# Attention with a gated Mish block: the last half groups normalised in a buffer of their own, leftover projections over three PSUM banks, and another order of the instructions

## The chip, the cores and the metric

The kernel runs on one core of a Trainium2 chip. The metric is the device time of one execution in microseconds (us). The kernel is one straight program: a planner written in Python decides, while the program is built, in which order each engine gets its instructions; on the chip the engines (TensorE = PE, ScalarE = ACT, VectorE = DVE, GpSimd = POOL, and the DMA queue of SyncE = SP) each run their own list in order and wait for each other by semaphores.

## The reference

The inputs are x (2048 x 640), weights of an attention with 32 heads of 20 columns, and weights of a dense block of 1536 columns. Only A_x is used as x.

```
x = A_x
g = sigmoid((x * gate_w).sum(-1, keepdims=True))
q, k, v = split((x @ wqkv), heads=32, width=20)
p = softmax(q @ k.T / sqrt(20))            # 32 heads, 2048 x 2048 each
a = concat(p @ v) @ wo
h = x @ w1 + b1
b = (h * tanh(softplus(h))) @ w2
out = g * a + (1 - g) * b
```

## The kernel before, in words

Four heads make a group g (0 to 7), 512 query columns a chunk c (0 to 3). The attention walks over the pairs (c, g): first chunks 0 and 1 for each g, then chunk 2 and chunk 3 through all g. A unit is 128 keys x 512 queries of one head. Three units fill a slot, three PSUM banks of scores; there are 683 slots, and two slots are in flight at a time (banks 0 to 2 and 3 to 5). Bank 6 (`ACC`) collects p @ v of the running group, bank 7 (`FB`) takes one projection task at a time.

The very last pair, (3, 7), is cut in two halves of 256 queries, which the code names (3, 7) and (3, 8), so that the first half can be finished while the second still runs.

A slot's way: PE writes its scores (`score_mms`, line 1197), ACT turns them into exp in an SBUF tile `ETS` (line 1219), PE multiplies them with V into `ACC` (`pv`, line 1456). V has a column of ones, so the row sums of the softmax arise in the same matmuls. In many slots one of the three units is taken off ACT: ACT then gets 128x1024 instead of 128x1536 elements, and DVE computes the third exp with integer and half-float tricks. That is an offloaded unit:

- line 1264 (`emit_x`): DVE reads the scores out of PSUM into an SBUF pad, 128x512, as an integer;
- lines 1328, 1332, 1336 (`close`): for a batch of up to four units, fraction, product and power, on 128x2048 elements for a full batch, 128x1024 for two and 128x512 for one (a batch of three as two plus one);
- `emit_off` then feeds both parts, "U" and "E", to PE as two V matmuls per unit.

Which slots lose a unit is decided by `choose`. It compares DVE's backlog as the planner knows it (`late`) with limits. Other work is spread around the slots: projections (`kq_task`, `pack_task`, `v_task`), the dense block (`h_task`, line 943, with Mish on ACT line 976 and DVE lines 998 and 1001; `b_task`, line 1017), the output projections (`p_task`, `part_task`, line 1041) and their mixing with the gate (`mix`, line 1047). `pick` takes the next task for PE in due order. `fill_up` puts in matmuls without use (`spin`, line 1735, and `repeat_s`) where PE would stream for too small a share of a window; `SPUN` and `STREAM` are the shares.

When a group's last matmul into `ACC` is done, `group_done` has DVE copy `ACC` to `OUNG` (line 1538), which frees `ACC` for the next group; the sums are inverted (line 1545), spread over partitions by DMA through DRAM (`SUMS`, `BCT`), and DVE multiplies (line 1506). The two last halves are normalised without DMA: copy, transpose, reciprocal, transpose, multiply on DVE (lines 1523 to 1531). The first half keeps its copy in `OUNG`, and needs `OUNG`, `BCT` and `RR` free, so the normalisation of group (3, 6), which uses the same buffers, is put ahead of it. The second half is read straight from PSUM.

For chunk 3 the sum over groups 0 to 5 is projected early (`part_task`, into `PART`, a part of `W2R`). Groups 6 and 7 follow: for the first 256 queries as `p_task` with rest=True (four tasks of two matmuls, each mixed by DVE into `HB` and stored), for the second 256 queries in four jobs after everything else, of which three are mixed by DVE, and one by ACT (line 1862) and POOL (line 1864). All of these four `p_task`s use bank 7.

Of the kernel before, what the change touches and what calls it, by code (L numbers as in the profile page):

```python
# [17 lines left out]
P = 128  # L18
# [5 lines left out]
NG = 8  # L24
# [4 lines left out]
NC = 4  # L29
CW = 512  # L30
NHC = 8
HW = 256
# [8 lines left out]
SLOT = 3  # L41
# [12 lines left out]
PASS = CW * COL  # L54
EXP = 1.335
STREAM = 0.5
SPUN = 0.65
EXP_PAIR = 0.908
WIDE = 0.60
QUICK = 0.335  # L60
# [39 lines left out]
WINDOW = 3.41  # L100
CALM = 3
# [8 lines left out]
THIN = 0.09  # L110
REFILL = 0.58
OVER = 0.2
CUTS = ((0, 256), (256, 256))

# [14 lines left out]
EXPONENT = 0x7C00  # L129
HALVES = 0x3800  # L130
WARM = 7
MORE = 8


# [108 lines left out]
def bass_gated_mix__softmax_full_mha__dense_activation_mish__prompt_kernel(  # L243
# [142 lines left out]
    def attention(pl, fast):  # L386
# [7 lines left out]
        soon = [deque() for _ in range(LANES)]  # L394
        norm = deque()
        acts = deque()
        now = {"step": -1, "open": None, "bank": False, "rate": 9.0}


        if fast:  # L400
# [1092 lines left out]
        def group_done(c, g, step, last):  # L1493
# [15 lines left out]
                    otn_read[c % 2] = []  # L1509

            if end:
                while norm:
                    norm.popleft()[1]()
                if (c, g) == groups[-1]:
                    flush(lambda: not any(soon))
                for at, w in ([cut[(c, g)]] if fast else [(n * HW, HW) for n in range(2)]):
                    cols = slice(at, at + w)
                    src, bc, rr = PS[:, ACC, cols], BC[:, cols], RR[:, at // 32:(at + w) // 32]
                    cost = w * COL * 2.6 + 0.09
                    if (c, g) != groups[-1]:  # L1520
                        held = OUNG[:, cols]
                        last = acc_free[0] = pl.add(
                            "dve", lambda e, src=src: e.tensor_copy(held, src), [last, oung_free[0]], cost=cost)
                        src = held
                    a = pl.add("dve", lambda e, src=src, bc=bc: e.transpose(bc, src), [last, bc_read[0]], cost=cost)
                    a = pl.add("dve", lambda e, bc=bc, rr=rr, w=w: e.reciprocal(rr, bc[:, 0:w:32]), [a, rr_read[0]], cost=0.15)
# [4 lines left out]
                    end_done.append(pl.add("dve", lambda e, src=src, bc=bc, to=to: e.tensor_tensor(  # L1531
                        to, src, bc, ALU.mult), [a, *reads()], cost=cost))
                oung_free[0] = bc_read[0] = rr_read[0] = otn_done[(c, g)] = end_done[-1]
                return
            while oung_free[0] == "busy":
# [2 lines left out]
            ev = dve(lambda e: e.tensor_copy(src, PS[:, ACC, :]), [last, oung_free[0]], WIDE)  # L1538
            oung_free[0] = "busy"
            acc_free[0] = ev  # L1540
            got = pl.add("sp", lambda e: e.dma_start(
                RR[:, :], OUNG[0:P:32, :].rearrange("j (r a) -> j r a", a=16)), [ev, rr_read[0]], "nr0", cost=0.55, tail=1.4 if place[(c, g)] else SLOW_LOAD)

# [16 lines left out]
        if fast:  # L1560
# [9 lines left out]
            for g in range(NG):  # L1570
                for c in range(NC):
                    due = slot_of(0, g, 4 * c)
                    if c or g:
                        if g == 0:
                            tasks.append(kq_task(1, g, c, due - 3))
                        if g < 2:
                            tasks.append(v_task(g, c, due - 1))
                        if g == 0:
                            tasks.append(kq_task(0, g, c, slot_of(1, 0, 0) - 5 if c < 2 else Q_AT + Q_STEP * (c - 2)))
# [37 lines left out]
            parts = [part_task(t, half, NSLOT - 26) for t in range(4) for half in range(2)]  # L1617
            parts += [p_task(NC - 1, t, half, NSLOT - 2, True) for t in range(last_t[0]) for half in range(2)]
            made = []
            for make, args in rest:  # L1620
                t = make(*args, 0)
# [39 lines left out]
        def load_flag(eng, handle):  # L1661
            flags[eng] = handle.value_load(FLAG[0:1, 0:1], min_val=0, max_val=1)

        def pick(limit):

            switch = SWITCH if pl.kind != "F" else 0
            if now["open"]:
                return now["open"] if pl.now["pe"] + now["open"].cost + switch <= limit else None
            free = bank_free.get(FB)
# [12 lines left out]

        def put(task):
            now["open"] = task
            if issue(task, FB):
                now["open"] = None
                tasks.remove(task)
                if fast and task is last_kv:
                    load_w1(FIRST)
                    load_w1(FIRST + 1)  # L1690
                    area[0] = 1
                if fast and task in q_tasks:
                    q_tasks.remove(task)
                    if not q_tasks:
                        load_wo()
# [301 lines left out]
```

## Time and profile before

| what | value |
|---|---|
| time, median of 3 runs | 791.36 us (791.05 to 792.82) |
| the profiled execution's own time | 791.27 us |
| its span in the profile | 789.4 us |
| busy: ACT, DVE, PE | 773.3, 748.6, 709.7 us |
| granted TensorE clock, mean | 0.997 |

The span runs from the first to the last instruction; the profiled execution took 1.87 us more than its span. Durations in the prediction come from this one execution. A duration of a single instruction includes its fill and drain, which overlap with its neighbours; the distance between two starts is what an instruction costs in a full queue.

### The profile page before, as it was taken

The page shows a single profiled execution, that of the slowest core. Times are in us where ns is not written, and L with a number is a line of the kernel's source. Part 1 is how long each engine was busy: PE and PEld are TensorE (multiplying, and loading weights), DVE is VectorE, ACT ScalarE, POOL GpSimd, SP SyncE. Part 2 cuts the span into 40 slices and gives each one's busy share as a digit, 9 for nine tenths or more (in the row PEclk, how much of TensorE's full clock was granted, in tenths as well). Part 3 has the DMA queues.
Part 4 walks back from the last instruction along what each step waited for, and adds up shares of the span by engine and source line. Part 5 has one row for each costly group of instructions (what it writes and reads, how often), then busy time and mean ns, then how long its engine had stood idle before and what let it go on. Part 6 is the DMA issues. An engine that isn't in the chain of part 4 may idle for free.

```text
span 789.4 us, 16424 instructions
## 1 busy us (share of the span) xinstructions
PE 709.7 (90%) x6649; PEld 262.4 (33%) x6690; DVE 748.6 (95%) x1313; ACT 773.3 (98%) x715; POOL 20.2 (3%) x21
## 2 busy tenths in 40 slices
PE   8899999889888888999999889999889899999985
PEld 4333333233323332233323233333333333333332
DVE  5899999999999999999999999999999999999995
ACT  6999999999999999999999999999999999999995
POOL 8100000000000000000000000000000000000000
PEclk9999999999999999999999999999999999999998
DMA  8221310212233221402112131202121213000101
GB/s 201 63 59 55 102 52 17 81 55 60 72 91 109 83 64 45 133 17 65 32 29 51 52 90 36 64 19 61 31 85 49 82 48 85 15 28 24 29 15 39
DMA packets 77799, 47.12 MB, mean 60 GB/s; under 512 B 23916, under 2 KB 73700, under 8 KB 77668
## 3 DMA queue, kind: packets, MB, share of 16 engines
q1 hardware_dynamic: 77316, 45.80, 21.0%
q8 instruction: 56, 0.92, 0.5%
q14 instruction: 27, 0.22, 0.1%
q10 hardware_dynamic: 288, 0.16, 0.1%
q0 software_dynamic: 112, 0.01, 0.1%
HBM read 36.26 MB, written 7.52 MB: 55 GB/s over the span
## 4 chain that ended last, share of the span: by engine, by line
ACT 90%; DVE 4%; PE 4%; DMA 1%; issue 0%; SPq 0%
ACT ETS L1219 87%; ACT REG L976 2%; PE PS L1197 1%; PE PS L1456 1%; ACT W2R L976 1%; DVE KT L1332 1%; DVE KT L1264 1%; DMA QT<-QS 1%; PE PS L555 0%; DVE QT L1264 0%; PE PS L1041 0%; SPq L651 0%; PE PS L738 0%; DVE HB L1047 0%; DVE HB L1264 0%
## 5 line engine op out<-in xcount | busy, mean ns | idle before, releaser
L1219 ACT ACTIVATE ETS<-PS 128x1024 bf16<-128x1024 f32 (+1 forms) x683 | 753.9, 1370 | 2.8 <-PE PS L1197 2.8
L1197 PE MATMUL PS<-QT,KT 32*128 32x512 bf16 (+1 forms) x2116 | 267.8, 378 | 57.1 <-ACT ETS L1219 48.1
L1456 PE MATMUL PS<-ETS,V_all 128*21 128x512 bf16 (+1 forms) x1699 | 161.7, 375 | 0.0
L1197 PEld LDWEIGHTS PS<-QT,KT 32*128 32x128 bf16 x2116 | 67.0, 91 | 281.6 <-ACT ETS L1219 255.9
L1264 DVE TENSOR_SCALAR PADS<-PS 128x512 int16<-128x512 f32 x97 | 66.0, 682 | 7.8 <-PE PS L1197 7.3
L1264 DVE TENSOR_SCALAR QT<-PS 128x512 int16<-128x512 f32 x102 | 69.5, 683 | 4.0 <-PE PS L1197 3.4
L1017 PE MATMUL PS<-W2R,HB 128*128 128x320 bf16 x384 | 68.5, 302 | 0.7 <-DVE HB L953 0.5
L1264 DVE TENSOR_SCALAR OTN<-PS 128x512 int16<-128x512 f32 x84 | 57.1, 681 | 0.6 <-PE PS L1197 0.5
L943 PE MATMUL PS<-XB,REG 128*128 128x256 bf16 x360 | 53.6, 274 | 2.3 <-DVE OUTT L1047 1.4
L1456 PEld LDWEIGHTS PS<-ETS,V_all 128*21 128x21 bf16 x1699 | 41.8, 90 | 41.4 <-issue 27.0
L1001 DVE TENSOR_TENSOR U<-U 128x1024 f16<-128x1024 f16 x72 | 49.0, 681 | 0.3
L1017 PEld LDWEIGHTS PS<-W2R,HB 128*128 128x128 bf16 x384 | 30.7, 97 | 32.4 <-issue 19.7
L943 PEld LDWEIGHTS PS<-XB,REG 128*128 128x128 bf16 x360 | 29.1, 97 | 25.8 <-issue 23.5
L953 DVE TENSOR_TENSOR HB<-PS,B1T 128x512 bf16<-128x512 f32 x48 | 32.7, 680 | 0.5 <-PE PS L943 0.3
L998 DVE TENSOR_SCALAR U<-U 128x1024 f16<-128x1024 f16 x72 | 29.9, 415 | 0.5
L1041 PE MATMUL PS<-WOQ,QT 128*128 128x320 bf16 x128 | 24.5, 302 | 2.3 <-DVE HB L1047 0.6
L1264 DVE TENSOR_SCALAR REG<-PS 128x512 int16<-128x512 f32 x38 | 25.7, 682 | 0.2
L1735 PE MATMUL PS<-KT 128*128 128x512 bf16 x79 | 24.1, 383 | 1.7 <-issue 1.1
L1041 PE MATMUL PS<-WOQ,OTN 128*128 128x320 bf16 x128 | 23.8, 302 | 0.2 <-issue 0.2
L815 PE MATMUL PS<-REG,XB 128*128 128x160 bf16 (+1 forms) x240 | 23.1, 234 | 0.0
L976 ACT ACTIVATE REG<-HB 128x1024 f32<-128x1024 bf16 x18 | 22.2, 1236 | 0.0
L660 PE MATMUL PS<-XB,REG 128*128 128x512 bf16 x69 | 20.3, 382 | 1.8 <-issue 1.1
(188 smaller groups left out, 816.0 us busy)
## 6 DMA issues: line engine op xcount, KB each, us to landing
REG<-in_B_w_dram SPq DMA_DIRECT2D x36, 320.0 KB, 3.2
BCT<-SUMS SPq DMA_DIRECT2D x124, 64.0 KB, 2.2
W2R<-in_B_w_dram SPq DMA_DIRECT2D x12, 320.0 KB, 3.8
KT<-KS SPq DMA_DIRECT2D x28, 128.0 KB
QT<-QS SPq DMA_DIRECT2D x112, 20.0 KB
QS<-WOQ SPq DMA_DIRECT2D x16, 128.0 KB, 1.7
KS<-OTN SPq DMA_DIRECT2D x16, 128.0 KB, 1.7
W2R<-in_B_w_dram SPq DMA_DIRECT2D x1, 1920.0 KB, 10.2
```

What stands on the lines that cost most here:

```text
L943: return lambda e, bank: e.matmul(PS[:, bank, i * HW:(i + 1) * HW], w1b(n1)[:, f, i * P:(i + 1) * P], xt(c)[:, f, cols], start=(f == 0), s ...
L953: ev = dve(lambda e: e.tensor_tensor(hb, PS[:, bank, :].rearrange("p (i t) -> p i t", i=2), bias, ALU.add), [last, b_load, *guarded, *b_re ...
L976: ex = pl.add("act", lambda e: e.activation(U, h, AF.Tanh, scale=0.5, bias=-MISH_AT), [ev, u_free[0]], cost=0.95)
L998: return lambda e: e.tensor_scalar(dst, src, *ops)
L1001: return lambda e: e.tensor_tensor(dst, one, two, ALU.mult)
L1017: return lambda e, bank: e.matmul(PS[:, bank, 0:HALF], HB[:, hc % 2, f, t * P:(t + 1) * P], W2[:, f, half * HALF:(half + 1) * HALF], start ...
L1041: return lambda e, bank: e.matmul(PS[:, bank, 0:HALF], otn(c, g, fast)[:, t * P:(t + 1) * P], WOG[:, g, half * HALF:(half + 1) * HALF], st ...
L1197: op = pl.add("pe", lambda e, i=i, g=real(g), tile=tile, j=j, cols=cols, c=c, of_q=of_q: e.matmul(scores(s)[:, i, cols], KT[32 * j:32 * j ...
L1219: e_op[s] = pl.add("act", lambda e: e.activation(ETS[:, s % NETS, 0:n, :], scores(s)[:, 0:n, :], AF.Exp, scale=SCALE, bias=LIFT if fast el ...
L1264: ev = dve_by(lambda e: e.tensor_scalar(block(batch["y"], n, I16), scores(s)[:, 2, :], SCALE * ULPS, BIAS, ALU.mult, ALU.add), [s_op[s], * ...
L1456: lasts[n] = pl.add("pe", lambda e, v=v, j=j, src=src[:, cols], of_q=of_q, count=count: e.matmul(PS[32 * j:32 * j + EW, ACC, of_q], v, src ...
L1735: pl.add("pe", lambda e: e.matmul(PS[:, bank, :], k[:, 0:P], k, start=True, stop=True), [free], cost=PASS, kind="S")
```

## The change

Three things are edited.

The two last halves get a buffer of their own: `U2`, which serves Mish before. The copy, the transposed sums and the reciprocals of the halves lie in `U2`, so neither half waits for `OUNG`, `BCT` or `RR`, and the pending normalisation of (3, 6) needs not stand ahead of the first half.

The projections that are put in after the last slot (`p_task`s still left over) no longer all use bank 7: `spot` hands out banks 7, 5 and 4 in turn. Before the last slot nothing changes there.

The order is set anew. `NUDGE` holds one number for every eight slots, which `choose` takes off DVE's backlog: a positive one lets it offload where it did not before. Limits of `pick` and of the offloading move too (`EAGER`, `LAG`), and the share up to which useless matmuls are put in falls (`SPUN`).

```diff
-SPUN = 0.65
+SPUN = 0.6
-EAGER = 20
+EAGER = 45
-LAG = 5
+LAG = 25
+DIRECT = 1
+FEW = 8
+PART_DUE = 26
+LAST_DUE = 2
+LEAD = 5
+NUDGE = [0, 0, 0, ..., -1, 0, 2, ..., 0.5, 3, 0, 0, 0, 3, 0, 1, 0.5, ..., 1]
...
-            late = max(0.0, pl.now["dve"] - pl.now["act"])
+            late = max(0.0, pl.now["dve"] - pl.now["act"]) - NUDGE[s // 8]
...
-                if not free_pads() or len(open_pads()) - waiting - 1 < 1 or tiles(*group) < 4:
+                if not free_pads() or len(open_pads()) - waiting - 1 < 1 or tiles(*group) < FEW:
...
             if end:
-                while norm:
-                    norm.popleft()[1]()
+                if not fast:
+                    while norm:
+                        norm.popleft()[1]()
...
+                    free = [bc_read[0], rr_read[0], oung_free[0]]
+                    if fast:
+                        bc, rr, free = U2[:, CW:CW + w], U2[:, CW + HW:CW + HW + w // 32], [None] * 3
...
-                        held = OUNG[:, cols]
+                        held = U2[:, 0:w] if fast else OUNG[:, cols]
...
+            if fast and c == NC - 1 and g >= NG - DIRECT:
+                turned_in = [ev]
...
+        def spot():
+
+            if not fast or now["step"] < NSLOT:
+                return FB
+            bank = (FB, 5, 4)[now["spot"] % 3]
+            if bank not in spots:
+                spots.add(bank)
+                bank_free[bank] = e_op[NSLOT - 1 - (bank // SLOT + NSLOT - 1) % 2]
+            return bank
...
-            if issue(task, FB):
+            if issue(task, spot()):
+                now["spot"] += now["step"] >= NSLOT
```

`FEW`, `DIRECT`, `LEAD`, `PART_DUE` and `LAST_DUE` alter nothing by themselves: a half group has 8 tiles, and 8 is not below `FEW`; the branch of `DIRECT` is for chunk 3 and g of 7 or more, for which `group_done` has returned already; the other three have the values that stood in the code.

In the part of the program that runs, the number of offloaded units goes from 401 to 406, so that ACT has 407 slots of 128x1024 and 276 of 128x1536 instead of 402 and 281. DVE's pieces for them (line 1328, 1332, 1336 in the old numbering) change so:

| piece | 128x2048 | 128x1024 | 128x512 |
|---|---|---|---|
| fraction, line 1328 | 91 to 85 | 15 to 24 | 7 to 18 |
| product, line 1332 | 38 to 34 | 121 to 126 | 7 to 18 |
| power, line 1336 | 91 to 85 | 15 to 24 | 7 to 18 |

The useless matmuls of line 1735 go from 92 to 88, and the repeated score matmuls from 4 to 20. The numbers of all other instructions on every engine stay as they are; the first 127 slots lose the same units as before.

Three places show the new order. The first is the end of ACT's list; all rows are exp, `ETS` the tile that they write.

```order
L1219 ACTIVATE ETS<-PS 128x1536
L1219 ACTIVATE ETS<-PS 128x1024 x2
L1219 ACTIVATE ETS<-PS 128x1536
L1219 ACTIVATE ETS<-PS 128x1024 x2
L1219 ACTIVATE ETS<-PS 128x1536 x9
L1219 ACTIVATE ETS<-PS 128x1024
```

And ACT after the change (exp is line 1226 there):

```order
L1226 ACTIVATE ETS<-PS 128x1536
L1226 ACTIVATE ETS<-PS 128x1024 x3
L1226 ACTIVATE ETS<-PS 128x1536 x2
L1226 ACTIVATE ETS<-PS 128x1024 x2
L1226 ACTIVATE ETS<-PS 128x1536 x5
L1226 ACTIVATE ETS<-PS 128x1024
```

Two more units are offloaded among the last ten slots; before, the last ten had none (the very last slot has only two units).

The second place is the end of DVE's list. `OUNG` to `QT` is the normalisation, `W2R` the early part of the projections, `HB` the mixed output; the rows begin with the first half's copy.

```order
L1523 COPY OUNG<-PS 128x256
L1525 STREAM_TRANSPOSE BCT<-OUNG 128x256
L1526 RECIPROCAL RR<-BCT 128x8
L1527 STREAM_TRANSPOSE BCT<-RR 128x256
L1531 TENSOR_TENSOR QT<-OUNG,BCT 128x256
L1047 SCALAR_TENSOR_TENSOR W2R<-PS,GATE,XB 128x320
L1047 SCALAR_TENSOR_TENSOR HB<-PS,GATE,W2R 128x320 x3
L1525 STREAM_TRANSPOSE BCT<-PS 128x256
L1526 RECIPROCAL RR<-BCT 128x8
L1527 STREAM_TRANSPOSE BCT<-RR 128x256
L1531 TENSOR_TENSOR QT<-PS,BCT 128x256
L1047 SCALAR_TENSOR_TENSOR HB<-PS,GATE,W2R 128x320 x4
```

DVE after the change, from just behind the first half's five instructions (`U` is the buffer `U2`; `REG` and `OTN` hold the last batch of offloaded units; the line numbers are those of the new code):

```order
L1335 TENSOR_SCALAR REG<-OTN 128x2048
L1513 TENSOR_TENSOR QT<-OUNG,BCT 128x512
L1054 SCALAR_TENSOR_TENSOR W2R<-PS,GATE,XB 128x320
L1339 TENSOR_TENSOR REG<-REG,OTN 128x2048
L1343 TENSOR_SCALAR OTN<-OTN 128x2048
L1054 SCALAR_TENSOR_TENSOR W2R<-PS,GATE,XB 128x320
L1054 SCALAR_TENSOR_TENSOR HB<-PS,GATE,W2R 128x320 x2
L1536 STREAM_TRANSPOSE U<-PS 128x256
L1537 RECIPROCAL U<-U 128x8
L1538 STREAM_TRANSPOSE U<-U 128x256
L1542 TENSOR_TENSOR QT<-PS,U 128x256
L1054 SCALAR_TENSOR_TENSOR HB<-PS,GATE,W2R 128x320 x5
```

The multiply of (3, 6) (`QT<-OUNG,BCT` 128x512) stood ahead of the first half and now stands behind it; the last batch of offloaded units is worked behind the first half, where before all batches were done by then; and behind the closing normalisation five mixes follow instead of four.

The third place is the end of PE's list, from the last score matmuls on: `ETS`, `REG` and `OTN` times `V_all` is p @ v, `WOQ` the output projection, `KT` a matmul without use.

```order
L1197 MATMUL PS<-QT,KT 128x256 x4
L1041 MATMUL PS<-WOQ,QT 128x320 x4
L1456 MATMUL PS<-ETS,V_all 21x256 x16
L1041 MATMUL PS<-WOQ,QT 128x320 x2
L1735 MATMUL PS<-KT 128x512
L1041 MATMUL PS<-WOQ,QT 128x320 x8
```

And PE after the change:

```order
L1204 MATMUL PS<-QT,KT 128x256 x4
L1048 MATMUL PS<-WOQ,QT 128x320 x2
L1463 MATMUL PS<-REG,V_all 21x256 x8
L1463 MATMUL PS<-ETS,V_all 21x256 x8
L1463 MATMUL PS<-OTN,V_all 21x256 x8
L1463 MATMUL PS<-ETS,V_all 21x256 x8
L1048 MATMUL PS<-WOQ,QT 128x320 x2
L1463 MATMUL PS<-ETS,V_all 21x256 x8
L1048 MATMUL PS<-WOQ,QT 128x320 x4
L1775 MATMUL PS<-KT 128x512
L1048 MATMUL PS<-WOQ,QT 128x320 x8
```

The last batch of offloaded units (`REG`, `OTN`) now comes behind the last scores, and two of the four `p_task`s (the row of four) behind the last p @ v, where one stood before.

More of the change, by code (lines that the diff above doesn't have):

```diff
@@ L131 @@
 WARM = 7
+LEAD = 5
+NUDGE = [0, 0, 0, 0, 0, 0, 0, 0, 0, 0, 0, 0, 0, 0, 0, 0, 0, 0, 0, 0, 0, 0, 0, 0, 0, 0, 0, 0, 0, 0, 0, 0, 0, 0, 0, 0, 0, 0, 0, 0, 0, 0, 0, 0, 0, 0, 0, 0, 0, 0, 0, 0, 0, 0, 0, -1, 0, 2, 0, 0, 0, 0, 0, 0, 0, 0.5, 3, 0, 0, 0, 3, 0, 1, 0.5, 0, 0, 0, 0, 0.5, 1, -0.5, 0, 0, -0.5, 0, 1]
 MORE = 8
@@ L396, in attention @@
         acts = deque()
-        now = {"step": -1, "open": None, "bank": False, "rate": 9.0}
+        spots = {FB}
+        now = {"step": -1, "spot": 0, "open": None, "bank": False, "rate": 9.0}
         if fast:
@@ L1518, in group_done @@
                     src, bc, rr = PS[:, ACC, cols], BC[:, cols], RR[:, at // 32:(at + w) // 32]
+                    free = [bc_read[0], rr_read[0], oung_free[0]]
+                    if fast:
+                        bc, rr, free = U2[:, CW:CW + w], U2[:, CW + HW:CW + HW + w // 32], [None] * 3
                     cost = w * COL * 2.6 + 0.09
                     if (c, g) != groups[-1]:
[L1521 removed]
+                        held = U2[:, 0:w] if fast else OUNG[:, cols]
                         last = acc_free[0] = pl.add(
[L1523 removed]
+                            "dve", lambda e, src=src, held=held: e.tensor_copy(held, src), [last, free[2]], cost=cost)
                         src = held
[L1525 to L1526 removed]
+                    a = pl.add("dve", lambda e, src=src, bc=bc: e.transpose(bc, src), [last, free[0]], cost=cost)
+                    a = pl.add("dve", lambda e, bc=bc, rr=rr, w=w: e.reciprocal(rr, bc[:, 0:w:32]), [a, free[1]], cost=0.15)
                     a = pl.add("dve", lambda e, bc=bc, rr=rr, w=w: e.transpose(
@@ L1532, in group_done @@
                         to, src, bc, ALU.mult), [a, *reads()], cost=cost))
+                if fast:
+                    otn_done[(c, g)] = end_done[-1]
+                    return
                 oung_free[0] = bc_read[0] = rr_read[0] = otn_done[(c, g)] = end_done[-1]
@@ L1540, in group_done, with turn, run @@
             acc_free[0] = ev
+            if fast and c == NC - 1 and g >= NG - DIRECT:
+                turned_in = [ev]
+                def turn(cost, fn, deps):
+                    def run():
+                        turned_in[0] = pl.add("dve", fn, [turned_in[0], *deps()], cost=cost)
+                    norm.append((cost, run, lambda: turned_in[0]))
+                turn(WIDE + 0.03, lambda e: e.transpose(BC, src), lambda: [bc_read[0], *spread_last])
+                turn(0.25, lambda e: e.reciprocal(RR[:, :], BC[:, 0:CW:32]), lambda: [rr_read[0]])
+                turn(WIDE + 0.03, lambda e: e.transpose(
+                    BC.rearrange("p (a r) -> p a r", r=32), RR[:, :].unsqueeze(2).to_broadcast([P, CW // 32, 32])),
+                    lambda: [])
+                norm.append((WIDE, lambda: times(src, turned_in), lambda: turned_in[0]))
+                return
             got = pl.add("sp", lambda e: e.dma_start(
@@ L1616, in attention @@
             rest += mixed(bs(7), ps(2))
-            parts = [part_task(t, half, NSLOT - 26) for t in range(4) for half in range(2)]
-            parts += [p_task(NC - 1, t, half, NSLOT - 2, True) for t in range(last_t[0]) for half in range(2)]
+            parts = [part_task(t, half, NSLOT - PART_DUE) for t in range(4) for half in range(2)]
+            parts += [p_task(NC - 1, t, half, NSLOT - (LAST_DUE, LAST_DUE, 2)[t], True) for t in range(last_t[0]) for half in range(2)]
             made = []
```

6 lines of the change are left out of this document (3 added, 3 removed).

## The prediction

> **What bounds the kernel now.** I read the page's busy times first, then the chain of work that ended last, then busy time by windows, then the exp groups by form.
>
> ```profile
> span 789.4 us, 16424 instructions
> PE 709.7 (90%) x6649; PEld 262.4 (33%) x6690; DVE 748.6 (95%) x1313; ACT 773.3 (98%) x715; POOL 20.2 (3%) x21
> ACT 90%; DVE 4%; PE 4%; DMA 1%; issue 0%; SPq 0%
> ACT ETS L1219 87%; ACT REG L976 2%; PE PS L1197 1%; PE PS L1456 1%; ACT W2R L976 1%; DVE KT L1332 1%; DVE KT L1264 1%; DMA QT<-QS 1%; PE PS L555 0%; DVE QT L1264 0%; PE PS L1041 0%; SPq L651 0%; PE PS L738 0%; DVE HB L1047 0%; DVE HB L1264 0%
> core 0: us, PE busy (x) PEld busy (x) DVE busy (x) ACT busy (x) POOL busy (x), PEclk, DMA share, GB/s
> 20.00:775.00 755.00, 686.43 (x6412) 250.67 (x6449) 732.79 (x1282) 753.22 (x696) 2.35 (x4) 1.00 0.20 56
> 775.00:789.40 14.40, 6.56 (x108) 2.99 (x97) 5.57 (x13) 6.06 (x6) 0.86 (x1) 0.85 0.18 52
> ACT ETS L1219 <- PE PS L1197: 2.8, 6, 1.0
> L1219 ACT ACTIVATE ETS<-PS 128x1536 bf16<-128x1536 f32 x281 | 446.8, 1621 | 2.2 <-PE PS L1197 2.2
> L1219 ACT ACTIVATE ETS<-PS 128x1024 bf16<-128x1024 f32 x402 | 441.4, 1195 | 0.6 <-PE PS L1197 0.6
> ```
>
> ACT is the chain: 90% of it. Between 20 and 775 us ACT idles 755.00 - 753.22 = 1.78 us; in all, exp waited for scores 2.8 us, in six places. So the program lasts as long as ACT's list, plus the start, plus what follows the last exp. DVE idles 755.00 - 732.79 = 22.2 us in the same stretch: it is almost full, but not the limit.
>
> **What an offloaded unit is worth to ACT.** A slot without its third unit takes 1621 - 1195 = 426 ns less (the two forms above; fill and drain are in both and drop out). Five more such slots give 5 x 0.426 = 2.13 us. ACT has no other instruction more or less.
>
> **What it costs DVE.** Prices are distances between starts in a full queue.
>
> ```profile
> 765.73 0.68 DVE L1332 TENSOR_TENSOR OTN<-OTN,PADS 128x1024 f16<-128x1024 f16 x1
> 766.33 0.68 DVE L1264 TENSOR_SCALAR OTN<-PS 128x512 int16<-128x512 f32 x1
> 766.93 0.68 DVE L1336 TENSOR_SCALAR PADS<-PADS 128x2048 int16<-128x2048 int16 x1
> 767.53 0.55 DVE L1047 SCALAR_TENSOR_TENSOR W2R<-PS,GATE,XB 128x320 f32<-128x320 f32 x1
> ...
> 768.72 1.22 DVE L1332 TENSOR_TENSOR OTN<-OTN 128x2048 f16<-128x2048 f16 x1
> 769.87 0.55 DVE L1047 SCALAR_TENSOR_TENSOR W2R<-PS,GATE,XB 128x320 f32<-128x320 f32 x1
> 770.34 0.68 DVE L1336 TENSOR_SCALAR OTN<-OTN 128x2048 int16<-128x2048 int16 x1
> 438.94 0.42 DVE L998 TENSOR_SCALAR U<-U 128x1024 f16<-128x1024 f16 x1
> 439.27 0.69 DVE L1328 TENSOR_SCALAR QT<-QT 128x2048 int16<-128x2048 int16 x1
> L1332 DVE TENSOR_TENSOR OTN<-OTN 128x512 f16<-128x512 f16 x2 | 0.8, 417 | 0.0
> L1336 DVE TENSOR_SCALAR QT<-QT 128x512 int16<-128x512 int16 x2 | 0.6, 288 | 0.0
> ```
>
> Reading a unit out of PSUM costs 766.93 - 766.33 = 0.60; fraction or power 0.60 on 2048 elements and 439.27 - 438.94 = 0.33 on 1024; the product 0.60 on 1024 and 769.87 - 768.72 = 1.15 on 2048; a mix 770.34 - 769.87 = 0.47. A queued instruction hides some 0.08 of its duration (0.68 against 0.60), so the pieces of 512 are estimated at 0.29 - 0.08 = 0.21 and 0.42 - 0.08 = 0.34. The sum over the table of pieces: five readings 3.0; fraction and power, each -6 x 0.60 + 9 x 0.33 + 11 x 0.21 = 1.68, together 3.36; product -4 x 1.15 + 5 x 0.60 + 11 x 0.34 = 2.14. DVE gets 8.5 us more, into a stretch that has 22.2 us idle and becomes 2.1 us shorter. Its idle would be about 11.6 us. By the sum it fits; whether it fits at each place is the question of the rivals.
>
> Half of this comes from cutting batches smaller: 40 more instructions of the three kinds. By rows a cut costs 2 x 0.33 - 0.60 = 0.06 us, 2.4 us for 40. [...]
>
> Other edits inside the stretch cost nothing by my reading. PE has 755.00 - 686.43 = 68.6 us idle there; 4 useless matmuls go, 16 repeats come, and without that cover their price would be 16 x 0.13, since three run side by side (0.38 / 3 by the row of line 1735 below), 2.1 us. SP's list is reordered among the same transfers; the first 127 slots lose the same units, so the start stays.
>
> **The tail.** Call T the end of the last exp.
>
> ```profile
> 749.56 30.97 ACT L1219 ACTIVATE ETS<-PS 128x1024 bf16<-128x1024 f32 x27
> 780.12 0.86 PE L1456 MATMUL PS<-ETS,V_all 128*21 128x256 bf16 x16
> 780.58 0.10 PEld L1456 LDWEIGHTS PS<-ETS,V_all 128*21 128x21 bf16 x6 [0.25 <-ACT ETS L1219]
> 781.02 0.45 DVE L1525 STREAM_TRANSPOSE BCT<-PS 128x256 f32<-128x256 f32 x1 [0.24 <-PE PS L1456]
> 782.56 2.09 DVE L1047 SCALAR_TENSOR_TENSOR HB<-PS,GATE,W2R 128x320 bf16<-128x320 f32 x4
> 782.70 0.72 PE L1041 MATMUL PS<-WOQ,QT 128*128 128x320 bf16 x4 [0.59 <-DVE QT L1531]
> 783.77 1.26 ACTq L1073 DMA_DIRECT2D out_dram<-HB  x2
> 772.92 0.42 DVE L1523 COPY OUNG<-PS 128x256 f32<-128x256 f32 x1
> 774.92 0.55 DVE L1047 SCALAR_TENSOR_TENSOR W2R<-PS,GATE,XB 128x320 f32<-128x320 f32 x1
> ```
>
> T is 749.56 + 30.97 = 780.53. The last p @ v follow at 780.58, the transposes at 781.02, four mixes from 782.56 to 784.65, and the end at 789.4: 8.87 us behind T. The last p @ v wait for ACT, so the tail before 781.02 cannot shrink: other banks for leftover projections save nothing on the path. Behind the closing normalisation five mixes stand instead of four. The first before ran while PE did the four matmuls from 782.70 to 783.42, and then the three of the jobs; now two stand ahead of the three. Full spacing gives 782.56 + 4 x 0.47 + 0.55 = 784.99 against 784.65: +0.3 us, if the store follows as before. Bounds: -0.1 (all of it hidden behind the stores) and +0.8 (a whole mix more and a store late by one issue).
>
> The new batch near the end must be done before that. Its last unit's scores can be written when the exp two slots ahead ends: counting back from T with 0.92 for a short and 1.35 for a long exp (13 and 14 of them make the 30.97 above), that is T - 0.92 - 5 x 1.35 - 2 x 0.92 = T - 9.5, and DVE may read them at about T - 9.0. What then stands in DVE's list: reading 0.60, mix 0.47, the first half's five instructions 774.92 - 772.92 = 2.00, fraction 0.60, multiply 0.60, mix 0.47, product 1.15, power 0.60, mix 0.47: 6.96. It ends near T - 2.0; the transposes come at T + 0.5 behind two mixes. Some 1.5 us of reserve: no cost, but the cover is thin, and each us of DVE lateness beyond it is a us of the end.
>
> **The sum.** 791.27 (the profiled execution's own time) - 2.13 + 0.3 = 789.44. That execution lies 0.09 below the median of the runs, so the forecast as a median is 789.5 us, 0.23% less. ACT's 1.78 us idle is taken as unchanged: 1.0 us of it falls into 20 to 40 us, which nothing touches; the other 0.8 could go, or grow.
>
> ```profile
> 20.00:40.00 20.00, 17.68 (x196) 7.08 (x194) 16.30 (x31) 19.00 (x19) 2.35 (x4) 1.00 0.21 62
> 441.07 0.40 PE L1456 MATMUL PS<-REG,V_all 128*21 128x512 f16 x4 [1.22 <-DVE OUNG L1538]
> 441.84 4.62 ACT L1219 ACTIVATE ETS<-PS 128x1536 bf16<-128x1536 f32 x4 [0.17 <-PE PS L1197]
> L555 PE MATMUL PS<-ETS 128*128 128x512 bf16 x7 | 3.2, 630 | 1.2 <-DVE ETS L541 1.2
> L1735 PE MATMUL PS<-KT 128*128 128x512 bf16 x79 | 24.1, 383 | 1.7 <-issue 1.1
> ```
>
> **Rivals.** A difference of 0.2%, 1.58 us, is about what a measurement of this kernel can tell from no change; so 789.78 and 792.94 are the borders.
>
> *The gain is eaten (28%).* At a group's change the first p @ v of the new group waits until DVE has copied `ACC`; scores stand behind it in PE's list. At 441 us PE waited 1.22 us so, and 0.17 of it reached ACT. With 8.5 us more in DVE's list such copies come later. Six such stalls of 0.17, 1.0 us, on 789.5 give 790.5: no change that can be told. For it: the windows leave DVE 3% idle now and 1.5% then. Against: the five units are spread, two of them into the last ten slots, where DVE's last batch was done at 771.02, 9.5 us before T.
>
> *DVE becomes the bound (11%).* `NUDGE` lets DVE be up to 3 us later than the planner's limit. If at a group's change the copy is 1.2 us later still, the wait has no slack left and ACT loses all of it: from three such places (3.6 us) on the kernel is slower than before. Priced with half of the 8.5 us on the path, 4.3, it is 793.8. For it: the 1.22 us at 441. Against: over a whole kernel that wait cost ACT little, and DVE's smaller pieces leave more places between which a copy can go.
>
> *The clock (5%).* Fewer useless matmuls could lower the granted clock, which was 1.00 in every window from 20 to 775 us. The seven matmuls of line 555 at the start took 630 ns against 383 for the same shape later, 1.64 times. If PE ran so through 10 us, its 9.1 us of work (686.43 of 755) would take 14.9: 4.9 us more, 794.4. Against: only 4 of 92 go, 16 repeats come. [...]
>
> The forecast itself has 56%. Its own range: -2.13 with the 0.8 of idle gone and no mix paid gives 788.4, with 0.1 hidden and some reading error 788.2; 0.8 in the tail and 0.6 more idle give 790.6.
>
> **Chances.** Of the 56%, 50 lie under 789.78 and 6 above. Of the 28%, 2 under, 25 between, 1 above the upper border. The other two, 11 and 5, are slower. Faster 52%, within 31%, slower 17%. The range 788.2 to 793.4 reaches over the forecast, the eaten gain and the lower part of the DVE case; out of it stay the clock, most of the DVE case and some 5% below.
>
> **What would show it.** Right: ACT busy down by about 2.1 us in the profile after, 276 and 407 exps, ACT's wait for scores near 2.8 us, last exp's end near 778.4, 9.2 us behind it, DVE's idle between 20 and the last exp near 12 us. Wrong: ACT's waits for scores grown by over 1 us with DVE named behind PE's waits (line 1538's successor), a clock below 1.00 in a window, or more than 10 us behind the last exp because the batch in `REG` and `OTN` came late.

## The result and the profile after

| | before | after |
|---|---|---|
| median of 11 runs each, us | 792.01 (791.05 to 792.94) | 789.37 (788.87 to 790.64) |
| profiled execution, us | 791.27 | 789.46 |
| its span, us | 789.4 | 787.6 |
| end of the last exp, T | 780.53 | 778.51 |
| span behind T | 8.87 | 9.09 |

The ratio after to before is 0.9969, 95% interval 0.996 to 0.9977: 1.8 to 3.2 us less. The two profiled executions differ by 1.81 us, as the prediction's sum does (1.83), and lie at the small end of that interval. The median of 789.37 us is closer to the forecast of 789.5 than the change is to its forecast: the forecast was counted from 791.36 us for the kernel before, and its 11 runs here came out at 792.01. That the two differences cancel is luck.

The page of the changed kernel, its windows (columns: PE, PEld, DVE, ACT, POOL busy, granted clock, DMA share, GB/s), its wait of exp for scores, and its exp groups by form:

```profile
span 787.6 us, 16572 instructions
PE 721.0 (92%) x6711; PEld 264.4 (34%) x6711; DVE 754.4 (96%) x1358; ACT 771.0 (98%) x715; POOL 20.3 (3%) x21
ACT 93%; PE 3%; DVE 3%; issue 0%; ACTq 0%
20.00:775.00 755.00, 697.99 (x6499) 252.79 (x6497) 737.78 (x1325) 753.05 (x698) 2.46 (x4) 1.00 0.20 56
ACT ETS L1226 <- PE PS L1204: 2.8, 5, 1.0
L1226 ACT ACTIVATE ETS<-PS 128x1024 bf16<-128x1024 f32 x407 | 443.2, 1191 | 0.8 <-PE PS L1204 0.8
L1226 ACT ACTIVATE ETS<-PS 128x1536 bf16<-128x1536 f32 x276 | 439.0, 1615 | 2.2 <-PE PS L1204 2.0
```

ACT's busy time fell by 773.3 - 771.0 = 2.3 us, exp still waits 2.8 us, and the clock is 1.00: ACT's list is shorter and nothing has eaten that. DVE has 755.00 - 737.78 = 17.2 us idle left.

The end of the program, in the timeline of the changed kernel (start, duration, engine, line, operation; in brackets the idle time before it and what ended that):

```profile
744.29 34.22 ACT L1226 ACTIVATE ETS<-PS 128x1536 bf16<-128x1536 f32 x31
775.50 0.69 DVE L1343 TENSOR_SCALAR OTN<-OTN 128x2048 int16<-128x2048 int16 x1
778.53 0.43 PE L1463 MATMUL PS<-ETS,V_all 128*21 128x256 bf16 x8
778.64 0.55 DVE L1054 SCALAR_TENSOR_TENSOR HB<-PS,GATE,W2R 128x320 bf16<-128x320 f32 x1 [0.81 <-PE PS L1048]
779.11 0.44 DVE L1536 STREAM_TRANSPOSE U<-PS 128x256 f32<-128x256 f32 x1
779.24 0.72 PE L1048 MATMUL PS<-WOQ,QT 128*128 128x320 bf16 x4 [0.29 <-DVE HB L1054]
780.64 2.37 DVE L1054 SCALAR_TENSOR_TENSOR HB<-PS,GATE,W2R 128x320 bf16<-128x320 f32 x5
```

T is 744.29 + 34.22 = 778.51. The last batch is done at 776.19, 2.3 us ahead of T. The transposes begin 0.60 behind T (0.49 before), and the five mixes end at 783.01, 4.50 behind T (4.12 before). Four projection matmuls run side by side with the normalisation, at 779.24: these are the two leftover projections, on banks of their own.

### The profile page after: what moved, and what is told of

Read it like the earlier page. It is cut to its first block, busy times and chain, and to the rows that moved or that the text cites. A ratio compares the mean times of both kernels' runs of the same rounds, so it can differ in the third digit from the quotient of the medians.

```text
span 787.6 us, 16572 instructions
## 1 busy us (share of the span) xinstructions
PE 721.0 (92%) x6711; PEld 264.4 (34%) x6711; DVE 754.4 (96%) x1358; ACT 771.0 (98%) x715; POOL 20.3 (3%) x21
## 4 chain that ended last, share of the span: by engine, by line
ACT 93%; PE 3%; DVE 3%; issue 0%; ACTq 0%
ACT ETS L1226 91%; ACT REG L983 2%; ACT W2R L983 1%; PE PS L1204 1%; PE PS L1463 1%; PE PS L562 0%; DVE HB L1054 0%; PE PS L1048 0%; PE PS L745 0%; PE PS L758 0%; PE PS L606 0%; DVE W2R L1054 0%; PE PS L950 0%; DVE QT L1271 0%; DVE QT L1513 0%
## 5 line engine op out<-in xcount | busy, mean ns | idle before, releaser
L1463 PE MATMUL PS<-ETS,V_all 128*21 128x512 bf16 (+1 forms) x1690 | 166.5, 375 | 0.5 <-DVE OUNG L1552 0.5
L1271 DVE TENSOR_SCALAR PADS<-PS 128x512 int16<-128x512 f32 x89 | 60.5, 683 | 6.8 <-PE PS L1204 6.5
L1271 DVE TENSOR_SCALAR QT<-PS 128x512 int16<-128x512 f32 x94 | 64.0, 683 | 2.2 <-PE PS L1204 1.6
L1271 DVE TENSOR_SCALAR OTN<-PS 128x512 int16<-128x512 f32 x89 | 60.4, 681 | 0.7 <-PE PS L1204 0.4
L1271 DVE TENSOR_SCALAR REG<-PS 128x512 int16<-128x512 f32 x49 | 33.3, 683 | 0.7 <-PE PS L1204 0.5
L1271 DVE TENSOR_SCALAR KT<-PS 128x512 int16<-128x512 f32 x40 | 27.3, 683 | 0.3
L667 PE MATMUL PS<-XB,REG 128*128 128x512 bf16 x80 | 23.2, 383 | 0.2 <-DVE WOQ L676 0.2
L1463 PE MATMUL PS<-QT,V_all 128*21 128x512 f16 x197 | 22.8, 384 | 0.4 <-DVE OUNG L1552 0.4
```

Source lines behind the costliest of these rows:

```text
L1271: ev = dve_by(lambda e: e.tensor_scalar(block(batch["y"], n, I16), scores(s)[:, 2, :], SCALE * ULPS, BIAS, ALU.mult, ALU.add), [s_op[s], * ...
L1463: lasts[n] = pl.add("pe", lambda e, v=v, j=j, src=src[:, cols], of_q=of_q, count=count: e.matmul(PS[32 * j:32 * j + EW, ACC, of_q], v, src ...
```

## The experiments

### Tail edits and order, each alone

Four kernels take the changed one apart. In `tail_only` the order goes back, and the buffer and the banks stay:

```diff
-SPUN = 0.6
+SPUN = 0.65
-EAGER = 45
+EAGER = 20
-LAG = 25
+LAG = 5
-NUDGE = [0, 0, 0, ..., 1]
+NUDGE = [0] * 100
```

> The changed kernel with the old table (NUDGE zero, SPUN 0.65, EAGER 20, LAG 5): 401 offloaded units as before, only the buffer of the halves and the three banks are new. Theory (the gain is ACT's five shorter exps, the tail edits save nothing by themselves): within 0.3 us of before, ratio 1.000, ACT busy 773.3. Rival (the gain lies in the tail edits): 2 us and more less than before, ratio 0.997.

In `order_only` the order stays, the halves use `OUNG`, `BCT` and `RR` again with the pending normalisation ahead, and all leftover projections use bank 7:

```diff
-                if not fast:
-                    while norm:
-                        norm.popleft()[1]()
+                while norm:
+                    norm.popleft()[1]()
...
-                        held = U2[:, 0:w] if fast else OUNG[:, cols]
+                        held = OUNG[:, cols]
...
-            if not fast or now["step"] < NSLOT:
+            if True:
                 return FB
```

> The changed kernel's order table (406 offloaded units) with the halves normalised in the old buffers and the leftover projections on bank 7 alone. ACT's list is 2.1 us shorter, but three leftover projections stand behind the last p @ v and share one bank, so each waits for the mix before it, and that mix waits for the closing normalisation. Theory A (only the exps count): 2.1 us less than before, ratio 0.997. Theory B (the new order needs the tail edits): two waits of a mix and a matmul, about 1 us each, and two more mixes of 0.47 us; the gain is gone, ratio 0.999 to 1.002, the last exp at 778.5 us and 11 to 12 us behind it.

`one_bank` has only the last of these three edits, `no_u2` only those of the buffer.

> The changed kernel with the leftover projections on bank 7 alone; all instructions and their order as in the changed kernel, only one bank fewer. Theory (behind the last p @ v the second leftover projection waits for the mix of the first, at about 2.6 us behind the last exp, and the eight closing matmuls stand behind it on PE): 1.0 to 1.5 us more than the changed kernel, ratio to before 0.998 to 0.999, and about 10.3 us from the last exp to the end. Rival, as the prediction had it (other banks save nothing on the path): the same time as the changed kernel, ratio 0.997.

> The changed kernel with the halves in the old buffers again (the multiply of (3, 6) ahead of the first half), the three banks kept: three leftover projections behind the last p @ v instead of two, six mixes behind the closing normalisation instead of five. Theory (a mix costs 0.47 us there, and three banks hold three projections): 0.5 to 0.8 us more than the changed kernel, ratio to before 0.998. Rival (the buffer saves nothing): as the changed kernel, 0.997.

| kernel | median, us | ratio to before (95%) | T | span behind T |
|---|---|---|---|---|
| tail_only | 791.53 | 1.000 (0.9992 to 1.0009) | 780.40 | 9.2 |
| order_only | 793.06 | 1.0011 (1.0 to 1.0021) | 778.03 | 13.1 |
| one_bank | 790.99 | 0.9988 (0.9979 to 0.9997) | 778.10 | 10.5 |
| no_u2 | 790.82 | 0.9983 (0.9974 to 0.9992) | 778.64 | 10.3 |
| after | 789.37 | 0.9969 (0.996 to 0.9977) | 778.51 | 9.1 |

T and the span are of one profiled execution each. Two expectations were too low: 11 to 12 us behind T for `order_only`, 0.5 to 0.8 us over the changed kernel for `no_u2`. Every kernel with the new order has T near 778; the tail edits decide what follows. With the old order they are worth nothing: the last mix of `tail_only` ends 4.13 us behind T, that of the kernel before 4.12. With the new one, from 793.06, the buffer alone brings 2.1 us, the banks alone 2.2, both 3.7.

Why the new order needs them is seen in the timeline of `order_only`, PE and then DVE:

```profile
778.43 0.40 PE L1463 MATMUL PS<-ETS,V_all 128*21 128x256 bf16 x8
779.15 0.45 PE L1048 MATMUL PS<-WOQ,QT 128*128 128x320 bf16 x2 [0.32 <-DVE HB L1054]
781.14 0.65 PE L1048 MATMUL PS<-WOQ,QT 128*128 128x320 bf16 x2 [1.55 <-DVE HB L1054]
782.44 0.71 PE L1048 MATMUL PS<-WOQ,QT 128*128 128x320 bf16 x2 [0.65 <-DVE HB L1054]
...
780.54 0.54 DVE L1054 SCALAR_TENSOR_TENSOR HB<-PS,GATE,W2R 128x320 bf16<-128x320 f32 x1
781.83 0.55 DVE L1054 SCALAR_TENSOR_TENSOR HB<-PS,GATE,W2R 128x320 bf16<-128x320 f32 x1 [0.74 <-PE PS L1048]
783.19 0.55 DVE L1054 SCALAR_TENSOR_TENSOR HB<-PS,GATE,W2R 128x320 bf16<-128x320 f32 x1 [0.81 <-PE PS L1048]
785.03 1.47 DVE L1054 SCALAR_TENSOR_TENSOR HB<-PS,GATE,W2R 128x320 bf16<-128x320 f32 x3 [1.28 <-PE PS L1048]
```

Three projections are left behind the last p @ v (778.43), and with one bank each waits for the mix that reads the one before it. The mixes stand in DVE's list behind the whole normalisation, so PE waits 1.55 and 0.65 us for DVE, DVE 0.74, 0.81 and 1.28 us for PE, in turn. The last mix ends at 786.50, 8.47 behind T. Not all of this is the bank: from 780 to 785 us the granted clock was 0.66 in this execution, and two projection matmuls that took 0.45 us at 779.15 took 0.65 and 0.71 there. In `one_bank` two are left, and one such turn:

```profile
780.81 1.75 PE L1048 MATMUL PS<-WOQ,QT 128*128 128x320 bf16 x10 [1.55 <-DVE HB L1054]
782.33 1.47 DVE L1054 SCALAR_TENSOR_TENSOR HB<-PS,GATE,W2R 128x320 bf16<-128x320 f32 x3 [0.48 <-PE PS L1048]
```

The last mix ends at 783.80, 5.70 behind T against 4.50 in the changed kernel: of the wait of 1.55 us, 1.2 come out there. The medians differ by 1.6. In `no_u2` the banks are there and the old buffers put everything behind the first half later; six mixes follow the normalisation instead of five, and it begins 0.98 behind T instead of 0.60:

```profile
779.62 0.44 DVE L1533 STREAM_TRANSPOSE BCT<-PS 128x256 f32<-128x256 f32 x1
781.15 2.83 DVE L1054 SCALAR_TENSOR_TENSOR HB<-PS,GATE,W2R 128x320 bf16<-128x320 f32 x6
```

The last mix ends at 783.98, 5.34 behind T against 4.50: 0.38 from the later start and 0.47 for a mix. The medians differ by 1.45 (by the ratios to before, 1.1); of the rest, 0.13 is a later T, and 0.33 lies behind the last mix (788.9 - 783.98 = 4.92 against 787.6 - 783.01 = 4.59) and was not taken apart. That stretch scatters by itself: in the traces of this section and of the other orders it lies between 4.6 and 5.1 us.

### Do the useless matmuls hold the clock?

`nospin` leaves out all 88 matmuls of line 1775, `halfspin` every second one. Both leave out only work without use.

```diff
-            pl.add("pe", lambda e: e.matmul(PS[:, bank, :], k[:, 0:P], k, start=True, stop=True),
+            pl.add("pe", lambda e: None if pl.prefix == 'f_' else e.matmul(PS[:, bank, :], k[:, 0:P], k, start=True, stop=True),
```

> The changed kernel with its 88 matmuls without use left out, everything else in its place. Theory of the clock (they keep the granted clock up): a granted clock under 1.00 in the windows where they stood, 300 to 420 and 740 to 755 us, and 3 us or more slower than the changed kernel. Rival (the clock holds without them, PE has time to spare): the same time within 0.3 us, ratio to before 0.997.

> The changed kernel with every second of its 88 matmuls without use left out (44 stay). Leaving all out cost 9.9 us, with a clock of 0.58 to 0.76 in five windows of 10 us. Theory A (the clock falls at single places where the share of work is too small, and half the matmuls keep it at some of them): 3 to 6 us more than the changed kernel. Theory B (half is enough everywhere): the same time within 0.4 us, clock 1.00. Theory C (all are needed): 8 to 10 us more.

`nospin` took 799.23 us, ratio 1.0094 (1.0081 to 1.0107), 9.9 us more than the changed kernel. Its wait of exp for scores, the four of its windows of 5 us with the lowest clock, and the first of these windows for the changed kernel and for `halfspin`, in this order:

```profile
ACT ETS L1226 <- PE PS L1204: 10.5, 18, 1.1
250.00:255.00 5.00, 4.21 (x30) 0.84 (x32) 4.52 (x8) 4.69 (x5) 0.00 (x0) 0.50 0.02 2
405.00:410.00 5.00, 4.17 (x28) 1.03 (x28) 4.00 (x9) 4.06 (x4) 0.00 (x0) 0.52 0.00 0
435.00:440.00 5.00, 5.00 (x36) 1.36 (x33) 4.10 (x9) 3.43 (x4) 0.00 (x0) 0.57 0.04 11
760.00:765.00 5.00, 5.00 (x41) 1.25 (x42) 4.07 (x8) 3.42 (x4) 0.00 (x0) 0.64 0.00 0
```

```profile
250.00:255.00 5.00, 4.90 (x43) 1.40 (x41) 4.97 (x9) 5.00 (x6) 0.00 (x0) 1.00 0.02 2
```

```profile
250.00:255.00 5.00, 4.16 (x38) 1.13 (x38) 5.00 (x10) 5.00 (x6) 0.00 (x0) 1.00 0.02 2
```

Without them the granted clock is under 1.00 in twelve windows of 5 us, between 0.50 and 0.82; in the first one shown PE does 30 matmuls instead of 43, and exp waits 7.7 us longer. The falls are at 245 to 260, 325 to 335, 405 to 420, 430 to 440 and 755 to 765 us, not all of them where the expectation had them. They follow the places of the matmuls that were left out: nearly all of the 88 stand from 240 to 260, from 310 to 340 and from 390 to 430 us, a few near 750. In the kernel before the clock was 1.00 from 780 to 784.9 us and 0.50 from 785.1 to 787.5, and 0.50 is also the lowest window of `nospin`. If its clock, too, stood at one of these two values at any time, a window of 0.64 had 0.50 for 3.6 of its 5 us, and the means of the twelve windows add up to an estimated 41 us at 0.50: 10.2, 6.8, 10.2, 6.8 and 6.8 in the five falls. `halfspin` took 789.0 us (788.71 to 789.92), ratio 0.9966 (0.9953 to 0.9979): as the changed kernel, with 38 matmuls in the window and still 1.00, as in every window of 5 us between 20 and 780 us (0.998 as the mean of the whole execution). So the fall from 92 to 88 cost no clock here, and half as many hold it; how few would, between none and 44, no run shows.

### Is DVE's idle time room?

The prediction's sum laid 8.5 us into 22.2 us of idle. `before_dve19` adds, without the planner knowing, 20 multiplies that touch nothing else, one every 29 slots from slot 127; each took 524 ns, and DVE's busy time rose by 6.4 us (0.36 of it a memset of their buffer at the start). `after_dve19` is the same in the changed kernel, with 6.0 us.

```diff
+    IDLER = sb("IDLER", [P, 360], FP32)
...
+            if s >= 127 and s // 29 != idle[-1]:
+                idle[1:] = [s // 29]
+                op = Op("dve", lambda e: e.tensor_tensor(IDLER[:, :], IDLER[:, :], IDLER[:, :], ALU.mult), [idle[0]], None)
+                pl.ops.append(op)
+                idle[0] = op
```

> The kernel before with 20 additional multiplies of 128x360 on DVE, one in about every 29 slots from slot 127 on, that nobody reads; an estimated 0.45 us each, 9.0 us in all, put in after the order was set, so that nothing makes room for them. Theory (8.5 us more on DVE are free, since it idles 22.2 us between 20 and 775 us): the same time as before within 0.4 us, ratio 1.000, DVE busy up by 9 us, ACT's wait for scores under 3.5 us. Rival (DVE has no room where it is needed): half of it reaches ACT, 4 us more, ratio 1.005.

> The changed kernel with 20 additional multiplies on DVE, as in the run on the kernel before. Theory (DVE's order was set with no room left, and the last batch stands 1.5 us ahead of the closing transposes): 2 us or more over the changed kernel, ratio to before 0.9995 and above. Rival (DVE still has 17 us idle and hides it): within 0.5 us of the changed kernel, ratio 0.997.

`before_dve19` took 795.07 us, ratio 1.0033 (1.002 to 1.0046), 2.7 us more than before, between the theory (0.4) and the rival (4); `after_dve19` 792.24, ratio to before 1.0005 (0.9996 to 1.0015), 2.9 us more than the changed kernel. So 0.4 to 0.5 of each added microsecond of busy time came out at the end, although DVE had 22 and 17 us idle. The profiled execution of `before_dve19` was its longest (796.08), that of `after_dve19` its shortest (790.87). In `before_dve19` exp's wait, two windows and what ended PE's and ACT's idle time there:

```profile
ACT ETS L1221 <- PE PS L1199: 5.6, 9, 1.0
440.00:445.00 5.00, 3.78 (x28) 0.74 (x28) 4.14 (x7) 3.91 (x4) 0.00 (x0) 0.63 0.09 21
445.00:450.00 5.00, 5.00 (x40) 1.68 (x33) 3.41 (x8) 3.61 (x4) 0.00 (x0) 0.69 0.04 8
441.56 0.61 PE L1463 MATMUL PS<-REG,V_all 128*21 128x512 f16 x4 [1.22 <-DVE OUNG L1545]
448.13 7.80 ACT L1221 ACTIVATE ETS<-PS 128x1536 bf16<-128x1536 f32 x7 [0.91 <-PE PS L1199]
```

It is the place of the prediction's first rival, and here ACT loses time there. But PE waits 1.22 us for DVE's copy of `ACC` in the kernel before too; what differs is the clock, 0.63 and 0.69 here, 1.00 there. Two rows of Mish on ACT stand on either side of the place; first in the kernel before, then in `before_dve19`:

```profile
433.67 1.22 ACT L976 ACTIVATE REG<-HB 128x1024 f32<-128x1024 bf16 x1
458.12 1.07 ACT L976 ACTIVATE REG<-HB 128x1024 f32<-128x1024 bf16 x1
...
434.15 1.22 ACT L978 ACTIVATE REG<-HB 128x1024 f32<-128x1024 bf16 x1
461.23 1.07 ACT L978 ACTIVATE REG<-HB 128x1024 f32<-128x1024 bf16 x1
```

ACT is 0.48 us late ahead of the place, 3.11 behind it, and 4.93 at T (785.46). So 2.6 us went at this place, with the clock down, and 1.8 us behind it, where no window of 5 us up to 785 us is under 1.00. In `after_dve19` no such window is under 1.00 at all, and T (779.92) is 1.41 later than in the changed kernel. So late DVE work costs ACT time without any fall of the clock, 1.8 and 1.4 us in these two traces; in one of them a fall came on top.

Whether the fall at 441 us is also what makes part of the executions of before longer, and whether more work for PE there prevents it, the next pair asks. It repeats the score matmuls of slots 386 and 390, three times each (12 matmuls), so that PE has more to do there:

```diff
+                if fast and step + 2 in (386, 390):
...
+                    for _ in range(3):
+                        repeat_s(step + 2)
```

> The kernel before with its scores of slots 386 and 390 written three times more (twelve matmuls), into PE's pauses ahead of and at the group change at 441 us, where PE waits 1.22 us for DVE's copy. Nothing else moves. Theory (in part of its executions the kernel before loses 1.5 us because the clock falls at this place, which the profiled one did not show; this is the part of the gain that the five exps don't give): the runs lose their upper half near 792.6, the median is 791.2, ratio 0.998 to 0.999. Rival (the spread has another cause): the spread stays, ratio 1.000.

> The kernel before with the 20 additional DVE multiplies (which alone cost 2.7 us and showed a clock of 0.63 to 0.69 from 440 to 450 us) and with the same twelve repeated score matmuls. Theory (the 9 us of DVE work cost little by themselves, the fallen clock at this place was nearly all of it): within 0.8 us of before, no window under 1.00. Rival (DVE's lateness itself costs it): 2 us and more slower than before, ratio 1.0025 and above.

`before_warm` took 792.92 us, ratio 1.0014 (1.0005 to 1.0023): slower, not faster. No 5 us window between 20 and 785 us was under 1.00, and exp's wait went from 2.8 to 3.4. Its Mish rows beside the place begin at 433.59 and 459.33 us, 0.08 earlier and 1.21 later than in the kernel before: the repeats cost this by themselves, as I read it because they stand ahead of scores that were wanted. Its clearest row of ACT (the wait was 0.17 in the kernel before):

```profile
443.05 16.42 ACT L1219 ACTIVATE ETS<-PS 128x1536 bf16<-128x1536 f32 x15 [0.57 <-PE PS L1197]
```

`before_dve19_warm` took 796.18, ratio 1.0044 (1.0032 to 1.0056), with a clock of 0.85 and 0.81 between 440 and 450 us, where it was 0.63 and 0.69 without the repeats, and a wait of 5.2. Both times came out against the theory. But since the repeats cost 1.2 us of their own, neither run shows that the clock at 441 us costs the kernel before nothing.

### Other orders

`table1` and `table3` keep the changed kernel's tail and have other numbers in `NUDGE`.

```diff
-LAG = 25
+LAG = 5
-PART_DUE = 26
-LAST_DUE = 2
+PART_DUE = 20
+LAST_DUE = 3
```

This is `table1` beside its `NUDGE`: 408 offloaded units, four closing mixes instead of five, 85 useless matmuls. `table3` has `SHIFT = 0.3` instead of 0.2, 409 units, five mixes, 109 useless matmuls.

> The changed kernel with other numbers in NUDGE, LAG 5, LAST_DUE 3 and PART_DUE 20: 408 offloaded units (the changed kernel has 406, before 401), four mixes behind the closing normalisation as before the change instead of five, 85 matmuls without use and 8 repeats. Theory (ACT's list and the tail set the end): 2 x 0.43 for the exps and 0.4 for the mix, 1.2 us less than the changed kernel, ratio to before 0.995. Rival (DVE is full at 406): ACT's waits for scores grow by over 1 us and it is no faster than the changed kernel, ratio 0.997 or more.

> The changed kernel with yet other numbers in NUDGE and SHIFT 0.3: 409 offloaded units, 109 matmuls without use. Theory (ACT's list sets the end): 3 x 0.43, 1.3 us less than the changed kernel, less or more what its tail has (five mixes behind the closing normalisation would keep it at that), ratio to before 0.995. Rival (DVE is full at 406): ACT's waits for scores grow by over 1 us and the ratio stays at 0.997 or more.

`table1` took **787.75 us** (787.72 to 788.32), ratio 0.995 (0.9937 to 0.9963); `table3` 788.19 (787.89 to 789.14), ratio 0.9958 (0.9945 to 0.9971). In `table1` exp's wait, the last exps and the last mixes are

```profile
ACT ETS L1226 <- PE PS L1204: 2.4, 4, 1.0
767.58 9.58 ACT L1226 ACTIVATE ETS<-PS 128x1024 bf16<-128x1024 f32 x8
779.19 2.09 DVE L1054 SCALAR_TENSOR_TENSOR HB<-PS,GATE,W2R 128x320 bf16<-128x320 f32 x4
```

T is 777.16, 1.35 earlier than in the changed kernel: 2 x 0.426 for two units more and 0.4 less waiting are 1.25. Its tail is 785.9 - 777.16 = 8.74, 0.35 shorter than 9.09, with a mix less. In `table3` T is 776.50, 2.02 earlier than in the changed kernel, and its five mixes end 4.50 behind T as there. Exp waits 2.4 us in both, so the rival (DVE is full at 406) fell. `table1` beats both kernels.

## Why the prediction was right, and where it was not

**ACT's list sets the end, 2.13 us for five units: right.** T came 2.02 earlier (2.13 counted from the first exp, which began at 9.39 instead of 9.28) and ACT's busy time fell by 2.3. So close a hit is partly luck: T lies 771.2 us behind the first exp in the two traces with the old order (before, `tail_only`) and 768.7 to 769.2 in five with the new one (after, `order_only`, `one_bank`, `no_u2`, `halfspin`), so 1.9 to 2.5 us. What an exp overlaps with the next drops out of the 426 ns, as the prediction had it: in the trace of before the next exp starts 0.904 us (128x1024) and 1.331 us (128x1536) behind one's start in the median, 0.29 less than the mean duration in both forms. Idle of ACT in the stretch went from 1.78 to 755.00 - 753.05 = 1.95, against "unchanged". `table1`, with seven units more than before, moved T by 3.37: 7 x 0.426 = 2.98 and 0.4 of waits.

**The tail, +0.3: right in its sum.** The last mix ends 4.50 behind T instead of 4.12, 0.38 later (forecast 0.34), and the span behind T grew by 9.09 - 8.87 = 0.22. The term of a fifth mix is borne out by `table1`, which has four and a tail 0.35 shorter. Transposes were seen at T + 0.60 (forecast 0.5) and the last batch's end at T - 2.3 (forecast 2.0).

**"Other banks for leftover projections save nothing on the path": wrong.** The step reasoned from the trace of before, where one leftover projection stands behind the last p @ v. The new order leaves more: with one bank the changed kernel takes 1.6 us more, and then more than half of the gain is gone. What the step left out is the wait of one leftover projection for the mix of the one before it, which stands behind the whole normalisation: 1.55 us on PE, 1.2 us at the last mix. The +0.3 already took the banks in, since it let the mixes run in full spacing, so the number held and the reason for it didn't. For the same cause the price of the buffer, 1.1 to 1.45 us with three banks, was not seen: read against before the buffer saves nothing (`tail_only`, 1.000), read against the new order it keeps a mix and a late start off the end.

**DVE's 8.5 us fit into its idle: the outcome right, the argument too weak.** DVE's busy time between 20 and 775 us rose by 737.78 - 732.79 = 5.0 us (5.8 in the whole span) and its idle is 17.2, not 11.6. The traces show why less than 8.5: the durations of all DVE instructions add up to 11.6 us more, but 71 more of them than before begin under the end of the one ahead (1202 instead of 1131), not only the 45 added ones, and each such overlap hides 0.08 us. So 5.8 of the 11.6 us were hidden, and 5.8 came out as busy time. ("Half of this" for the cutting is a slip of the prediction: its own rows give 2.4 of 8.5.) But idle time was no measure of room: 6.4 us of unplanned work cost 2.7 and 2.9 us beside 22 and 17 us of idle. The change's own extra work, about as much, did not come late for ACT, whose wait stayed 2.8 us: it was placed by the planner, the 20 multiplies at even distances. Of the rival of the eaten gain it is shown that late DVE work can reach ACT; that it does so by the copies at a group's change is not, since the wait of 1.22 us at 441 was no longer in `before_dve19`. In the changed kernel it did not happen.

**Edits in the stretch cost nothing; the clock: right.** The clock was 1.00 with 88, and with 44. The rival was of the right kind: without any, the loss is 9.9 us. But its price was too high: it took 4.9 us for 10 us of slow clock, and in `nospin` an estimated 41 us of it put T off by 8.74, some 2 us for each 10.

**What is left open.** The medians differ by 2.64 us, the profiled pair and the sum by 1.8. The median of before over 11 runs is 0.74 above its profiled execution, that of after 0.09 below. The mean granted clock, on record for each execution, says more than the two kernels with repeats. Of 69 executions of the kernel before that were taken beside the experiments, the 30 with a mean clock of 0.996 or less all took 792.0 us or more (median 792.57); the 39 others have a median of 791.47. All 11 of the changed kernel have 0.997 or more. So the upward scatter of before goes with the clock, and against its other executions the changed kernel gains 791.47 - 789.37 = 2.1 us, near the sum. Whether the lower clock makes these executions longer or follows from a delay in them, where it falls, and why the changed kernel is spared, is not settled: the one kept trace of before isn't among them.

## What to carry to other kernels

An edit at the end of a kernel has to be priced against the order that it will meet, not against the one in the old trace: here the buffer and the banks were worth nothing under the old order and 3.7 us under the new one (part of which is the lower clock in `order_only`), and either of the two changes alone, order or tail, gave no gain. Price work that the engine on the path loses by its own list, one unit at a time; that term held within the scatter of T, some 0.5 us. Don't take the idle time of an engine that is 97% full as room (here 6.4 us of work beside 22 us of idle cost 2.7 us): add a known amount of work to it and see what comes out.

## What the runs showed of the hardware

Forty-four useless matmuls, beside PE's real work, were enough for a granted clock of 1.00 in every window of 5 us between 20 and 780 us. With none the clock was 0.50 to 0.82 in twelve of them, at 9.9 us in all. It fell at 245 to 260, 325 to 335, 405 to 420, 430 to 440 and 755 to 765 us, where these matmuls had stood or close behind.

ACT's loss in `after_dve19` does not show as a wait. There exp's waits are 2.7 us (2.8 in the changed kernel), yet T is 1.4 later; ACT's busy time is 1.0 higher while the mean exp got shorter:

```profile
L1228 ACT ACTIVATE ETS<-PS 128x1024 bf16<-128x1024 f32 x407 | 434.5, 1157 | 0.7 <-PE PS L1206 0.7
L1228 ACT ACTIVATE ETS<-PS 128x1536 bf16<-128x1536 f32 x276 | 430.1, 1577 | 2.6 <-PE PS L1206 2.1
```

That is 34 and 38 ns less than the 1191 and 1615 ns of the changed kernel, 24.3 us over all 683 exps, while the busy time, which counts an overlap once, rose: so the exps overlapped less. `nospin` shows the same sign (1170 and 1597). I read it as exps that began later under their predecessor's end because scores came later; that reading was not tested by itself.
